# One planned order of instructions exchanged for another in a fused attention and SoLU kernel, with one GpSimd subtraction cut in two

## Chip, cores and metric

The kernel runs on one core of one Trainium2 chip. The metric is the device time of one execution in microseconds (us). Before the change it is 658.14 us, the median of 3 runs (658.04 to 658.26).

## What is computed

For 8 batches of 8 heads, 576 tokens and 64 features, causal attention with a decay that is summed along the sequence, and behind it a layer of width 1024 for each of the 4608 tokens:

```python
scores = scale * np.matmul(q, k.transpose(0, 1, 3, 2))
cum = np.cumsum(np.log(np.clip(f, 0.0001, 1.0)), axis=-1)
scores = np.where(causal, -1e9, scores + cum[:, :, :, None] - cum[:, :, None, :])
attn = softmax(scores)                      # with 1e-9 added to the sum
x = (attn @ v) as 4608 x 512                # all heads of a token side by side
h = x @ w_in                                # 512 -> 1024
solu = h * softmax(h)
ln = (solu - mean(solu)) / sqrt(var(solu) + 1e-6) * g_ln
out = ln @ w_out                            # 1024 -> 512
```

## The kernel before

**The pieces.** The 64 heads are worked on as 32 pairs (pair p is heads 2hp and 2hp+1 of batch p // 4). A pair's queries are cut into 5 tiles: 64 tokens, and four of 128. Query tile i sees the first 64 + 128 i keys, so scores are 64, 192, 320, 448 and 576 columns wide (the last in two parts of 288). Tiles 0 to 2 are "half 0" of a pair (320 tokens), tiles 3 and 4 "half 1". The layer works on 36 tiles of 128 tokens, numbered 0 to 35.

**High and low words.** Nearly every product is made from f16 words: an operand is split into a high word and the remainder, and three products (high by high, low by high, high by low) are added up. The first pairs are done in f32.

**One pair.** TensorE (PE) makes the scores in PSUM (`score_products`, L822, and L820 for the decay). VectorE (DVE) adds the mask and takes each row's maximum (L843), ScalarE (ACT) takes the exponential with its sum (L848), GpSimd (POOL) prepares the sum (L854), DVE its reciprocal (L855). ACT or POOL writes the high word of the normalized row (L504, L506), DVE the low one (L876), a transposing DMA from the SP queue turns both (L513), and PE multiplies with v (`values`, L925). ACT and DVE split that result into the two words of x (L935, L936).

**One layer tile** (`layer`). PE makes h in 8 steps of three 512-column products each (`product_in`, L956 to L958) into `hps`, two PSUM banks of which there is one copy. DVE takes the maximum (L967, L968), ACT the exponential (L970), DVE weighs it (L974); from then on `hps` is free for the next tile. POOL and ACT work out the variance (L978 to L980, L984, L988, L989), POOL normalizes (L994), ACT writes z's high word (L504), POOL subtracts to get the lower word (L998, 1024 columns in one instruction), a transposing DMA turns z, and PE makes 8 more steps of three products (`product_out`, L1026 to L1028). ACT evicts (L1058), SP stores. The names in the text: in7 is `product_in` of tile 7, out7 its `product_out`; one step of either is three products.

**What sets the order.** The Python code only records operations (`Plan.op`), each with its engine, an estimate of its duration, what it reads and writes. `Plan.schedule` then lists them: at every turn it takes, for each engine, the ready operation with the smallest rank in the table `RANK` (3576 numbers), and appends the one that can begin first. Each engine executes its part of that list in order. Where the model expects PE to stand idle and `FILLED` has a share for that time, blank products of 256 columns go into the gap (L1151); they are computed on nothing and keep PE busy. Six PSUM banks (`ps`) go round among scores, transposes, values and outputs.

```python
Z_LO = (3,) * 36                                   # 3 is POOL
op(Z_LO[n], {DVE: 1280, POOL: 2130}[Z_LO[n]], at, lambda: engine(Z_LO[n]).tensor_tensor(
    z16[:, :, 1], e2, z16[:, :, 0], ALU.subtract), [ek, zk_], [(*zk_, "l")], port=True)
FILLED = ((0.0, 300.0, 1.0), (690.0, 1000.0, 0.8)) # from, to in us of the plan, share to fill
best[e] = min((x for x in ready if x[0] <= t), key=lambda x: (x[1].due - ..., x[1].seq))
```

**The start.** The weights `w_in` come in four parts, each read as bits and split by ACT, DVE and POOL (L583, L597, L603, L619), while pairs 0 to 3 run their half 0. in0 needs half 0 of all four pairs. ACT also takes sums of squares of v (L684 on `vraw`) and of q and k (L684 on `raws`) of a batch, from which the scales of that batch's words are made; the first `raws` squared are those of batch 2.

Of the kernel before, what the change touches and what calls it, by code (L numbers as in the profile page):

```python
# [46 lines left out]
AFTER = (205.0, 135.0, 170.0, 70.0, 100.0)  # L47
# [9 lines left out]
TURN = (1100.0, 25.0, 1700.0, 6.0)  # L57
KEEP = 0.0
FILLED = ((0.0, 300.0, 1.0), (690.0, 1000.0, 0.8))
# [5 lines left out]
LANES = 8  # L65
WAIT = (0.0, 250.0, 60.0, 200.0, 0.0)

WHOLE, SCORE, TURNS, HALVES = range(4)
SWITCH = ((0.0, 120.0, 0.0, 120.0), (120.0, 0.0, 120.0, 120.0), (0.0, 120.0, 0.0, 120.0), (120.0, 120.0, 120.0, 0.0))
# [7 lines left out]
class Op:  # L77
    __slots__ = ("eng", "ns", "fn", "due", "deps", "users", "take", "keys", "left", "ready", "end", "tail", "seq", "dense", "port", "form", "layer")


class Plan:
# [10 lines left out]
    def op(self, eng, ns, due, fn, reads=(), writes=(), take=None, clear=(), tail=0.0, dense=True, port=False, form=0):  # L92
# [3 lines left out]
        o.eng, o.ns, o.fn, o.take, o.tail, o.seq, o.dense = eng, ns, fn, take, tail, len(self.ops), dense  # L96
        o.due = RANK[o.seq]
# [17 lines left out]
    def schedule(self):  # L115
        free, wire, order, gone, self.held = [0.0] * 5, 0.0, [], {}, {}
        form, port, half_clock, worked, lanes = 0, 0.0, True, 0.0, [0.0] * LANES
        todo = [[] for _ in range(5)]
        for o in self.ops:
            o.left, o.ready, o.users = len(o.deps), 0.0, []  # L120
            for d in o.deps:
                d.users.append(o)
            if not o.left:
                todo[o.eng].append(o)
        best = [None] * 5
        stale = set(range(5))
        for _ in self.ops:
            for e in stale:
                ready = []
                for o in todo[e]:  # L130
                    r = max(o.ready, free[e], port if o.port else 0.0)
                    if o.take:
                        places = self.pools[o.take[0][0]]
                        if len(places) < len(o.take):
                            continue
                        r = max(r, sorted(places)[len(o.take) - 1][0])
                    ready.append((r, o))
                best[e] = None
                if ready:
                    t = min(r for r, _ in ready) + WAIT[e]  # L140
                    best[e] = min((x for x in ready if x[0] <= t), key=lambda x: (x[1].due - (KEEP if e == PE and x[1].form == form else 0.0), x[1].seq))
            t, o = min((x for x in best if x), key=lambda x: x[0])
            stale = {PE, ACT, DVE, POOL, o.eng}
            todo[o.eng].remove(o)
            for k in o.take:
                place = min(self.pools[k[0]])
                self.pools[k[0]].remove(place)
                self.place[k] = place[1]
            self.place.update(zip(o.take, sorted(self.place[k] for k in o.take)))
            if o.eng == SP:  # L150
                t = max(t, lanes.pop(0))
                free[SP] = t + max(450.0, o.tail)
                wire = max(wire, t + 600.0) + o.ns
                o.end = max(t + 1900.0, wire + (TURN[2] if o.tail else 1300.0))
                lanes.append(o.end)
            else:
                ns = o.ns
                if o.eng == PE:
# [9 lines left out]
                free[o.eng] = t + ns  # L168
                o.end = t + ns
                if o.port:  # L170
                    port = o.end
# [1024 lines left out]
```

## Time and profile before

| | before |
|---|---|
| median of 3 runs | 658.14 us (658.04 to 658.26) |
| span of the profiled execution | 655.3 us |
| PE busy | 629.9 us (96%) |
| DVE busy | 553.4 us (84%) |
| ACT busy | 513.4 us (78%) |
| POOL busy | 400.5 us (61%) |
| DMA moved | 110.79 MB |

The span runs from the first instruction to the last of one execution that was recorded. That execution's own time is not given apart from its span; against the median of the timed runs it leaves 2.84 us that lie outside the span. A matmul's recorded end is modelled and lies about 0.16 us behind the start of the next, so a PE that is busy by the record can still hide short waits.

### The profile page before, as it was taken

How to read it: one execution, taken by the hardware profiler on the slowest of the kernel's cores; microseconds unless marked ns; L12 is line 12 of the kernel's file. 1: busy time of each engine (PE TensorE's matmuls, PEld its weight loads, DVE VectorE, ACT ScalarE, POOL GpSimd, SP SyncE). 2: the span in 40 equal slices, each digit the busy share in tenths (PEclk: the TensorE clock that was granted, in tenths of full speed). 3: DMA queues.
4: the chain of work that ended last, by engine and by line, in shares of the span. 5: the costliest groups of instructions: out<-in, count | busy, mean ns of one | idle time of the engine just before them, and what ended most of it. 6: DMA issues, size and time to landing. Idle time of an engine off the chain costs nothing. (4 is left out here: it accounts for less than half of the span.)

```text
span 655.3 us, 17355 instructions
## 1 busy us (share of the span) xinstructions
PE 629.9 (96%) x6312; PEld 343.7 (52%) x6312; DVE 553.4 (84%) x1644; ACT 513.4 (78%) x1290; POOL 400.5 (61%) x625
## 2 busy tenths in 40 slices
PE   5989999999999999999999999999999999999998
PEld 4655655555544456455455545555544554554445
DVE  6977999999999999999899888999999987874222
ACT  6998858978986987989888797888788887664433
POOL 3575762476767746876666667786677745555530
PEclk8999999999999999999999999999999999999999
DMA  8856128949897998999998989999769888686341
GB/s 338 332 176 221 55 65 207 176 76 227 185 197 150 193 230 138 206 171 214 185 214 199 187 146 210 217 181 191 148 96 167 150 155 126 138 148 129 74 97 48
DMA packets 262709, 110.79 MB, mean 169 GB/s; under 512 B 248288, under 2 KB 248736, under 8 KB 261600
## 3 DMA queue, kind: packets, MB, share of 16 engines
q1 hardware_dynamic: 262624, 109.69, 78.4%
q8 instruction: 49, 0.80, 0.5%
q14 instruction: 36, 0.29, 0.1%
HBM read 38.27 MB, written 9.66 MB: 73 GB/s over the span
## 5 line engine op out<-in xcount | busy, mean ns | idle before, releaser
L848 ACT ACTIVATE p<-p,nm 128x448 f32<-128x448 f32 (+4 forms) x208 | 132.8, 640 | 24.2 <-DVE nm L843 23.7
L956 PE MATMUL hps<-wi_h,x_h 128*128 128x512 f16 x288 | 109.8, 381 | 4.1 <-DVE e L974 3.8
L822 PE MATMUL ps<-qk 64*128 64x288 f16 (+9 forms) x1056 | 103.4, 306 | 10.4 <-DMA qk<-in_qk_dram 6.1
L957 PE MATMUL hps<-wi_l,x_h 128*128 128x512 f16 x288 | 109.3, 380 | 0.0
L958 PE MATMUL hps<-wi_h,x_l 128*128 128x512 f16 x288 | 109.3, 380 | 0.0
L1026 PE MATMUL ps<-wo_f,zz 128*128 128x512 f16 x280 | 106.7, 381 | 0.8 <-DMA zz<-z 0.8
L1027 PE MATMUL ps<-wo_f,zz 128*128 128x512 f16 x280 | 106.3, 380 | 0.0
L1028 PE MATMUL ps<-wo_f,zz 128*128 128x512 f16 x280 | 106.3, 380 | 0.0
L854 POOL TENSOR_SCALAR sm<-sm 128x2 f32<-128x2 f32 (+1 forms) x128 | 40.7, 318 | 105.7 <-ACT p L848 68.3
L843 DVE CUSTOM_DVE_ANT_0 p<-ps,mask 128x320 f32<-128x320 f32 (+4 forms) x208 | 96.7, 496 | 4.2 <-PE ps L820 2.2
L876 DVE SCALAR_TENSOR_TENSOR wo_p<-p,ri,wo_p 128x576 f16<-128x576 f32 (+1 forms) x112 | 95.3, 873 | 3.8 <-ACT wo_p L504 2.0
L998 POOL TENSOR_TENSOR z<-e,z 128x1024 f16<-128x1024 f32 x32 | 69.8, 2181 | 22.7 <-ACT z L504 22.1
L925 PEld LDWEIGHTS <-v 128*64 128x64 f16 x2520 | 70.0, 110 | 17.6 <-issue 15.9
L925 PE MATMUL ps<-t_p,v 128*64 128x128 f16 (+1 forms) x2520 | 77.0, 219 | 1.7 <-DMA t_p<-p16s 1.2
L967 DVE TENSOR_REDUCE st<-hps 128x1 f32<-128x1024 f32 x36 | 43.7, 1215 | 28.1 <-PE hps L958 28.0
L970 ACT ACTIVATE e<-hps,st,unscale 128x1024 f32<-128x1024 f32 x32 | 38.4, 1201 | 20.9 <-DVE st L968 19.1
L506 POOL TENSOR_SCALAR wo_p<-p,ri 128x576 f16<-128x576 f32 x56 | 45.2, 812 | 15.5 <-DVE ri L855 14.6
L974 DVE SCALAR_TENSOR_TENSOR e<-hps,e 128x1024 f32<-128x1024 f32 x36 | 43.7, 1214 | 11.1 <-ACT e L970 11.0
L822 PEld LDWEIGHTS <-qk 64*128 64x128 f16 x864 | 32.7, 94 | 36.1 <-issue 24.8
L820 PE MATMUL ps<-crow,pick 64*128 64x448 bf16 (+1 forms) x360 | 51.4, 276 | 0.0
L956 PEld LDWEIGHTS <-x_h 128*128 128x128 f16 x288 | 28.0, 97 | 39.9 <-issue 11.9
L984 ACT ACTIVATE junk<-e,st 128x1024 bf16<-128x1024 f32 x36 | 41.3, 1147 | 8.7 <-DVE e L974 8.5
(188 smaller groups left out, 1315.5 us busy)
## 6 DMA issues: line engine op xcount, KB each, us to landing
raws<-in_qk_dram SPq DMA_DIRECT2D x24, 576.0 KB, 4.9
vraw<-in_v_dram SPq DMA_DIRECT2D x8, 1280.0 KB, 7.2
out_dram<-y SPq DMA_DIRECT2D x35, 256.0 KB, 2.6
qk<-in_qk_dram SPq DMA_DIRECT2D x8, 576.0 KB, 8.7
wo_raw<-in_w_in_dram SPq DMA_DIRECT2D x4, 1024.0 KB, 8.1
vraw<-in_w_out_dram SPq DMA_DIRECT2D x2, 1024.0 KB, 5.0
t_raw<-in_w_out_dram SPq DMA_DIRECT2D x2, 1024.0 KB, 4.9
t_p<-p16s SPq DMA_TRANSPOSE x84, 3.5
```

The source lines that it names most:

```text
L822: nc.tensor.matmul(dst, x[row(h), 0, q0:q0 + P], y[row(h), 1, cols], start=(n == 0), stop=False)
L843: op(DVE, R_NS[i] if n == 0 else 442, at[i][h] + STEPS[0], lambda i=i, h=h, n=n, a=a, e=e, x=x, m0=m0: nc.vector.tensor_tensor_reduce(home ...
L848: op(ACT, E_NS[i] + (0 if banked(p, i) or i == 4 else 28), at[i][h] + STEPS[1], lambda i=i, h=h, x=x: nc.scalar.activation(home(i, h), hom ...
L876: op(DVE, L_NS[j], at[j][g] + STEPS[4], lambda j=j, g=g, nq=nq, h16=h16, l16=l16, r1=r1: nc.vector.scalar_tensor_tensor(l16(), home(j, g, ...
L925: nc.tensor.matmul(o[row(h), a:a + n], v16[m][:, x, 2 * j + h], t[:, y, i + j if h else i - j], start=(j == 0 and c == 0), stop=(j == i an ...
L956: nc.tensor.matmul(hps[:, sl], x_h, wi_h[:, c, sl], start=(c == 0), stop=False)
L957: nc.tensor.matmul(hps[:, sl], x_h, wi_l[:, c, sl], start=False, stop=False)
L958: nc.tensor.matmul(hps[:, sl], x_l, wi_h[:, c, sl], start=False, stop=(c == NCC - 1))
L998: op(Z_LO[n], {DVE: 1280, POOL: 2130}[Z_LO[n]], at, lambda: engine(Z_LO[n]).tensor_tensor(z16[:, :, 1], e2, z16[:, :, 0], ALU.subtract), [ ...
L1026: nc.tensor.matmul(o, zz[:, a, 0, j], wo(0, k), start=(k == 0), stop=False)
L1027: nc.tensor.matmul(o, zz[:, a, 0, j], wo(1, k), start=False, stop=False)
L1028: nc.tensor.matmul(o, zz[:, a, 1, j], wo(0, k), start=False, stop=(k == NFC - 1))
```

## The change

1. `RANK` is gone. A table `ORDER` of 3716 numbers lists all operations; `schedule` cuts it into one fixed row per engine and goes through the rows with a new model of times. The model now has a delay for every pair of engines (`LATE_BY`), durations by operation (`TRACED`), a model of the DMA ring (`RING`, `ISSUE`), and one of DVE and POOL excluding each other for operations marked `port` (`BEHIND`, `HOLD`).
2. The subtraction for z's lower word is two POOL operations of 512 columns.
3. The three small POOL operations of `sums` and the two of `deviation` are recorded one by one, so that others can stand between them. They are the same instructions.
4. `FILLED` is 0 to 13.5 us in full and 13.5 to 60 us at 0.75; blank products are 135 (before 138).

```diff
-AFTER = (205.0, 135.0, 170.0, 70.0, 100.0)
+LATE_BY = ((205.0, 205.0, 205.0, 205.0, 205.0), (165.0, 135.0, 135.0, 180.0, 135.0), ...)
-FILLED = ((0.0, 300.0, 1.0), (690.0, 1000.0, 0.8))
+FILLED = ((0.0, 13.5, 1.0), (13.5, 60.0, 0.75))
-        o.due = RANK[o.seq]
+        o.hold = HOLD[eng == POOL] if ns > 360.0 or eng == DVE else ns
+        o.ns = TRACED.get((eng, round(ns, 1)), ns)
...
-                    best[e] = min((x for x in ready if x[0] <= t), key=lambda x: (x[1].due - ..., x[1].seq))
+        for n in ORDER:
+            rows[self.ops[n].eng].append(self.ops[n])
+                o = row[0]
+                t = max([free[e], *(d.end + (SAME[e] if d.eng == e != SP else LATE_BY[d.eng][e]) for d in o.deps)])
...
-            op(Z_LO[n], {DVE: 1280, POOL: 2130}[Z_LO[n]], at, lambda: engine(Z_LO[n]).tensor_tensor(z16[:, :, 1], e2, z16[:, :, 0], ALU.subtract),
-               [ek, zk_], [(*zk_, "l")], port=True)
+            for a in range(2):
+                op(POOL, 1085, at, lambda a=a: nc.gpsimd.tensor_tensor(z16[:, a, 1], e2[:, a], z16[:, a, 0], ALU.subtract), [ek, zk_], [(*zk_, "l", a)])
```

The products and their operands, the DVE and ACT instructions and the DMAs are the same; what differs is where they stand. Three places:

**ACT, in the start**, around the squares of `raws` (L684, now L695); `p` are exponentials of pairs 1 and 2, `t` copies of transposed tiles, `x_h` high words of x. Before:

```order
L848 ACTIVATE p_64,sm_94<-p_64,nm_86 128x192
L684 ACTIVATE junk,top_113<-raws 128x1152
L935 ACTIVATE x_h<-ps_145,scale_117 128x320
L684 ACTIVATE junk,top_113<-raws 128x1152 x2
L504 ACTIVATE t_1_p<-ps_145 128x256
```

Now:

```order
L859 ACTIVATE p_64,sm_94<-p_64,nm_86 128x192 x2
L946 ACTIVATE x_h<-ps_150,scale_117 128x320
L515 ACTIVATE t_1_p<-ps_147 128x384
L515 ACTIVATE t_1_p<-ps_150 128x256
L859 ACTIVATE p_65,sm_95<-p_65,nm_87 128x320 x2
```

Three of the four squares stood here and the fourth eleven rows further on; all four now stand behind the exponential of layer tile 0.

**DVE, layer tile 14**, from the maximum (L968, now L979) to the weighing that frees `hps` (L974, now L985); `wo_p`, `p16s` are words of attention rows. Before:

```order
L968 TENSOR_SCALAR st_143<-st_143,unscale_128 128x1
L855 RECIPROCAL ri_90<-sm_94 128x2
L787 SCALAR_TENSOR_TENSOR v_3_82<-vraw_76,scale_121,v_3_82 128x640
L876 SCALAR_TENSOR_TENSOR p16s_84<-p_65,ri_90,p16s_84 128x320
L876 SCALAR_TENSOR_TENSOR wo_p_1255<-p_67,ri_89,wo_p_1255 128x576 x2
L876 SCALAR_TENSOR_TENSOR p16s_84<-p_65,ri_90,p16s_84 128x320
L936 SCALAR_TENSOR_TENSOR x_l<-ps_150,x_h 128x320
L974 SCALAR_TENSOR_TENSOR e_102,st_143<-hps,e_102 128x1024
```

Now:

```order
L979 TENSOR_SCALAR st_143<-st_143,unscale_128 128x1
L866 RECIPROCAL ri_90<-sm_94 128x4
L854 ISA p_66,nm_86<-ps_145,mask 128x448
L854 ISA nm_86 128x1
L854 ISA p_66,nm_86<-ps_147,mask 128x448
L854 ISA nm_86 128x1
L887 SCALAR_TENSOR_TENSOR wo_p_1250<-p_67,ri_89,wo_p_1250 128x576
L985 SCALAR_TENSOR_TENSOR e_102,st_143<-hps,e_102 128x1024
```

Six long instructions stood between; now there are three.

**POOL, layer tile 4**, from the normalization (L994, now L1001) on; `sm` are sums of exponentials, `v` a word of v. Before:

```order
L994 TENSOR_SCALAR e_102<-e_102,st_143 128x1024
L854 TENSOR_SCALAR sm_93<-sm_93 128x2
L998 TENSOR_TENSOR z_104<-e_102,z_104 128x2x512
L854 TENSOR_SCALAR sm_94<-sm_94 128x4
L506 TENSOR_SCALAR wo_p_1255<-p_67,ri_89 128x576
```

Now:

```order
L1001 TENSOR_SCALAR e_102<-e_102,st_143 128x1024
L1006 TENSOR_TENSOR z_104<-e_102,z_104 128x512
L865 TENSOR_SCALAR sm_93<-sm_93 128x2
L1006 TENSOR_TENSOR z_104<-e_102,z_104 128x512
L797 TENSOR_SCALAR v_3_82<-vraw_76,scale_119 128x640
```

The subtraction is in two, and the small sum of pair 4 has moved in between. In 18 of the 32 layer tiles that go this way, something stands between the halves.

## Rows read from the trace of the kernel before

**Rows 1.** The page's head: span, and each engine's busy time.

```profile
span 655.3 us, 17355 instructions
...
PE 629.9 (96%) x6312; PEld 343.7 (52%) x6312; DVE 553.4 (84%) x1644; ACT 513.4 (78%) x1290; POOL 400.5 (61%) x625
```

**Rows 2.** Busy time by stretch: length, engines, granted clock, DMA share.

```profile
core 0: us, PE busy (x) PEld busy (x) DVE busy (x) ACT busy (x) POOL busy (x), PEclk, DMA share, GB/s
13.70:18.70 5.00, 4.92 (x35) 3.30 (x36) 4.83 (x15) 4.81 (x9) 1.79 (x4) 0.50 1.01 407
...
20.00:49.40 29.40, 26.85 (x273) 18.56 (x268) 24.56 (x90) 28.59 (x84) 20.32 (x39) 1.00 0.66 235
...
60.00:100.00 40.00, 40.00 (x320) 24.33 (x317) 39.09 (x120) 29.01 (x70) 25.64 (x46) 1.00 0.27 90
60.00:500.00 440.00, 431.16 (x4513) 230.87 (x4510) 416.22 (x1265) 370.57 (x952) 291.25 (x438) 1.00 0.86 173
500.00:548.00 48.00, 45.72 (x557) 25.12 (x555) 41.16 (x134) 38.98 (x112) 29.76 (x42) 1.00 0.84 145
548.00:655.30 107.30, 104.05 (x825) 54.23 (x819) 51.67 (x115) 53.13 (x99) 46.34 (x69) 1.00 0.53 109
```

**Rows 3.** The same view for the blank products (L1151) alone: PE, PEld, clock.

```profile
0.00:13.70 13.70, 6.29 (x40) 4.72 (x40) 0.93 0.84 322
...
60.00:160.00 100.00, 4.04 (x29) 2.51 (x29) 1.00 0.60 138
```

**Rows 4.** Whom PE waited for, 60 to 548 us: total, times, longest.

```profile
PE hps L956 <- DVE e L974: 3.8, 4, 1.3
PE ps L822 <- DVE nm L843: 1.9, 4, 1.2
PE ps L822 <- ACT y L1058: 1.7, 1, 1.7
PE ps L925 <- DMA t_p<-p16s: 1.2, 2, 0.9
```

**Rows 5.** PE's timeline at five places: start, length, what, [idle before].

```profile
55.22 0.38 PE L956 MATMUL hps<-wi_h,x_h 128*128 128x512 f16 x1
...
198.59 1.12 PE L925 MATMUL ps<-t_p,v 128*64 128x64 f16 x36
199.65 0.39 PE L1026 MATMUL ps<-wo_f,zz 128*128 128x512 f16 x1
...
205.04 0.38 PE L956 MATMUL hps<-wi_h,x_h 128*128 128x512 f16 x1 [1.34 <-DVE e L974]
...
205.69 0.38 PE L956 MATMUL hps<-wi_h,x_h 128*128 128x512 f16 x1
...
309.27 0.38 PE L1028 MATMUL ps<-wo_f,zz 128*128 128x512 f16 x1
309.58 0.26 PE L822 MATMUL ps<-qk 64*128 64x64 f16 x6
...
312.73 0.72 PE L822 MATMUL ps<-qk 64*128 64x448 f16 x5 [1.66 <-ACT y L1058]
```

**Rows 6.** ACT's groups between 20 and 49.4 us: the squares of `raws`.

```profile
L684 ACT ACTIVATE junk<-raws 128x1152 bf16<-128x1152 f32 x4 | 4.6, 1158 | 0.0
```

**Rows 7.** DVE's groups by shape: busy us, mean ns of one, idle before.

```profile
L876 DVE SCALAR_TENSOR_TENSOR wo_p<-p,ri,wo_p 128x576 f16<-128x576 f32 x56 | 53.0, 968 | 1.4 <-POOL wo_p L506 1.4
...
L777 DVE SCALAR_TENSOR_TENSOR qk<-raws,scale,qk 128x576 f16<-128x576 f32 x48 | 41.3, 873 | 0.0
```

**Rows 8.** Four lines by themselves: least/median/largest ns of one.

```profile
L876 DVE SCALAR_TENSOR_TENSOR wo_p<-p,ri,wo_p x112: 655/801/2691, 103.9 to 595.5; 128x448 f16<-128x448 f32 x56, 128x576 f16<-128x576 f32 x56
...
L777 DVE SCALAR_TENSOR_TENSOR qk<-raws,scale,qk x48: 782/806/1675, 138.2 to 518.5; 128x576 f16<-128x576 f32 x48
...
L998 POOL TENSOR_TENSOR z<-e,z x32: 2122/2132/2619, 149.3 to 632.3; 128x1024 f16<-128x1024 f32 x32
...
L854 POOL TENSOR_SCALAR sm<-sm x128: 191/192/1647, 20.0 to 589.4; 128x2 f32<-128x2 f32 x96, 128x4 f32<-128x4 f32 x32
```

More of the change, by code (lines that the diff above doesn't have):

```diff
@@ L77 @@
 class Op:
-    __slots__ = ("eng", "ns", "fn", "due", "deps", "users", "take", "keys", "left", "ready", "end", "tail", "seq", "dense", "port", "form", "layer")
+    __slots__ = ("eng", "ns", "fn", "deps", "users", "take", "keys", "left", "ready", "end", "tail", "seq", "dense", "port", "form", "layer", "blocks", "hold")
 class Plan:
@@ new lines, in schedule @@
+        rows = [[] for _ in range(5)]
+        for n in ORDER:
+            rows[self.ops[n].eng].append(self.ops[n])
+        free, port, order, gone, last, self.held = [0.0] * 5, [0.0] * 5, [], {}, {}, {}
+        form, half_clock, worked, lanes, ring, drained = 0, True, 0.0, [0.0] * LANES, [], 0.0
+        for o in self.ops:
+            o.end = None
+        for _ in self.ops:
+            best = None
+            for e, row in enumerate(rows):
+                if not row or any(d.end is None for d in row[0].deps):
+                    continue
+                o = row[0]
+                t = max([free[e], *(d.end + (SAME[e] if d.eng == e != SP else LATE_BY[d.eng][e]) for d in o.deps)])
+                if o.take:
+                    places = sorted(self.pools[o.take[0][0]])
+                    if len(places) < len(o.take):
+                        continue
+                    t = max(t, places[len(o.take) - 1][0])
+                for k in o.keys:
+                    t = max([t, *(x + LATE_BY[f][e] for f, x in last.get(k, {}).items() if f != e)])
+                if o.port:
+                    t = max(t, port[POOL if e == DVE else DVE])
+                when = t + (BEHIND if o.port and e == POOL else 0.0)
+                if best is None or when < best[0]:
+                    best = when, t, o
+            _, t, o = best
+            e = o.eng
+            rows[e].pop(0)
+            for k, place in zip(o.take, sorted(n for _, n in sorted(self.pools["s"])[:len(o.take)])):
+                self.place[k] = place
+            for place in sorted(self.pools["s"])[:len(o.take)]:
+                self.pools["s"].remove(place)
+            if e == SP:
+                t = max(t, lanes.pop(0))
+                n, ns, issued = (o.blocks, o.blocks * RING[1], ISSUE[0] + ISSUE[1] * o.blocks + (ISSUE[2] if o.blocks > 128 else 0.0)) if o.tail else (max(1.0, o.ns / 120.0), o.ns * RING[2], ISSUE[3])
+                since = max(t + RING[3], drained)
+                drained = since + ns
+                ring = ring[-11:] + [(since, drained, n)]
+                free[SP], many = t + issued, 0.0
+                for a, z, n in reversed(ring):
+                    if many + n > RING[0]:
+                        free[SP] = max(free[SP], z - (RING[0] - many) / n * (z - a))
+                        break
+                    many += n
+                free[SP] += ISSUE[4]
+                o.end = drained + RING[4]
@@ L822, in products @@
                             nc.tensor.matmul(dst, x[row(h), 0, q0:q0 + P], y[row(h), 1, cols], start=(n == 0), stop=False)
[L823 removed]
+        ns = 8 + sum((16 if near else 10 if p < NAT * NPAIR else 8) * ((5.0 if p < NAT * NPAIR else 1.4) + 0.2084 * (cuts(i)[1 + (a > 0)] - a)) for i, a in pieces)
         op(PE, ns, at, products, [*((x, m, j) for x in ("qk", "qkl") for j in range(2)), *(("crow", a2, h) for h in range(2) if not near),
@@ L1138, in tile_kernel @@
     with tc.manual_schedule():
-        order, idle, busy = plan.schedule(), [], 8000.0
+        order, idle = plan.schedule(), []
+        busy = plan.writer[("const",)].end + LATE_BY[POOL][PE]
         for t, o in order:
```

113 lines of the change are left out of this document (35 added, 78 removed), and 289 rows, old and new, of tables (ORDER, RANK).

## The prediction, made before the changed kernel ran

> **What bounds the kernel.** I read the page's head first: of a span of 655.3 us PE is busy 629.9, DVE 553.4 [rows 1]. Averages over unlike stages don't say which engine to ask, so next the busy time by stretch [rows 2]. Three stages stand out. From 20 to 49.4 us ACT is busy 28.59 of 29.40 us: it sets the pace, and DVE has 4.84 us to spare there. From 60 to 500 PE is busy 431.16 of 440 and DVE 416.22: PE binds, and DVE is so close behind that PE stops wherever DVE is late. From 548 to the end PE is busy 104.05 of 107.3, and the missing 3.25 us are the last eviction and store: nothing but layer products, which an order can't shorten.
>
> So the end is PE's work plus the time in which PE does nothing useful. That time is of three kinds: the start, until in0 at 55.22 us [rows 5]; blank products, 4.04 us between 60 and 160 [rows 3]; and waits between 60 and 548, (440 - 431.16) + (48 - 45.72) = 11.1 us [rows 2], whose owners the list of waits names [rows 4].
>
> The useful work is the same after the change: row for row, every engine has as many instructions of each kind, except 3 fewer blanks and 32 more on POOL. Only idle time, blanks and the cost of switching can move, and whatever is moved changes the time about one for one. A change under 0.2% (1.3 us) I call no change, since a measurement can hardly tell it.
>
> **The start.** Four squares of `raws` leave ACT's saturated stretch: 4.6 us busy, plus four reads of the sum that mostly lie beside other work [rows 6]. Behind 60 us they cost nothing, since ACT is busy 29.01 of 40 us there [rows 2]; were that cover gone, 4.6 us. Nobody needs them early: they feed the scales of batch 2. SP loads two of the four `raws` later to match, behind the parts of w_out, past no transfer that in0 needs. What is late next is DVE: it can follow by its 4.84 idle us at most. Bounds 0 and -4.8; I take **-4.0**, near the upper end, because ACT has no idle time before the squares and DVE must do the same work to reach in0.
>
> Ahead of the first scores PE now gets 79 blanks instead of 40. Before, it stood idle after them and the granted clock from 13.70 to 18.70 was 0.50, the 1.2 GHz level, with PE busy 4.92 of 5.0 us [rows 2, 3]. If the clock stays up, up to 2.5 us of PE time fall away; but ACT (4.81 of 5.0) and DVE (4.83) are full in the same stretch and hide it: 0.
>
> **Blanks.** The other 56 stand before in0, and none behind 60 us. The 4.04 us between 60 and 160 fall away where PE would not have waited anyway. Bounds 0 and -4.0; **-2**, half, for want of a row that tells them apart.
>
> **Waits for `hps`**, 3.8 us in four places [rows 4]. in n+1 can't begin until DVE has weighed tile n. I listed what PE does between the end of in n and in n+1 at these four. One step of a layer takes 0.65 us (205.04 to 205.69), a half 0 of values 1.06 (198.59 to 199.65) [rows 5]; scores and half 1 of values I price by their columns at the same speed, as estimates.
>
> - After in6: 8 steps, tile-4 scores and a scale before; now also a half 0 of values and tile-1 scores: 7.1 to 8.7 us.
> - After in7: 8 steps and a half 0 before; now 8 steps, a half 1 and two sets of scores: 6.3 to 8.3.
> - After in14: 7.8 to 8.8.
> - After in25: 6 steps and a half 1 before, 8 steps and a half 1 now: 5.5 to 6.8.
>
> Each gains more than the mean wait of 0.95 us. After in14 DVE itself also gets to the weighing with three long instructions ahead of it instead of six. Bounds 0 and -3.8; **-3.0**.
>
> **The wait for a bank.** PE stood 1.66 us inside pair 17's 448-column scores until ACT had evicted out11's result [rows 5]. These scores now stand 8 steps of in14 and a half 1 of values later, some 6.8 us: **-1.5** (0 to -1.7).
>
> **Other waits**, 11.1 - 3.8 - 1.7 = 5.6 us. I can't follow them one by one through the new order; the bounds are -5.6 and +4. On average more PE work now stands between a half 0's last scores and its values (25.0 us against 21.4, by the same prices), but pair 30 has it cut from 16.5 to 10.3. **-1.5**.
>
> **Switching.** From a layer product to other work costs 0.31 us (309.27 to 309.58 [rows 5]) where a product otherwise takes 0.22. The order has 94 such exits to scores or values before, 77 now: 17 x 0.09 = **-1.5** (0 to -1.5).
>
> **New waits.** Handovers of `hps` become tighter after in19 (9.4 to 6.3 us), in26 (17.2 to 12.0) and in31 (5.2 to 4.7). At 0.95 us for a wait [rows 4], I take two: **+2**, with 0 and eight (+8) as bounds.
>
> **The halves.** DVE operations with two operands in SBUF are held up when POOL works: the 576-column L876 takes 968 ns on average, L777 of the same shape 873 [rows 7], while the median of the latter is 806 and single L876 reach 2691, about one L998 (2132) over its normal time [rows 8]. That is (968 - 806) x 56 + (873 - 806) x 48 = 12.3 us of DVE's time. L998 is the longest thing that POOL does, so halving it can give back 6 us at most; I expect 3. It gets no term of its own: it shortens DVE, and where that shows at the end it is in the waits above.
>
> The Trainium skill ("SBUF — State Buffer", section "SBUF: two separate sides") says why: VectorE and GpSimd share a port pair under an exclusive lock for a whole instruction, not by splitting bandwidth. The 2691 ns agree. By that rule the halves are worth their 3 us of DVE, at most 643.6 us if all of it reached the end; by shared bandwidth nothing, and the sum stays as below.
>
> For POOL the halves cost a second fixed price, of which the nearest row is the smallest sum, 0.19 us [rows 8]: 32 x 0.19 = 6.1 us of an engine that is busy 61% [rows 1]. A longer way of z to its product is hidden by the PE work between in n and out n, 18 us or more in each of the 32 tiles by the same prices.
>
> **The sum.** -4.0 - 2 - 3 - 1.5 - 1.5 - 1.5 + 2 = -11.5. That is against the profiled execution: 655.3 - 11.5 = 643.8 us of span. The median of the runs is 2.84 us above that span; I keep the difference: **646.6 us**. With all good ends it is -21.4 (636.7), with the bad ends of new and other waits and nothing gained +12.
>
> **Rivals.**
>
> 1. *The start is caught up.* DVE is busy 94.6% from 60 to 500; if it can't run 4 us further ahead, PE waits for it in small pieces later. The time is 650.6. For it speaks rows 2, against it that DVE itself idles in the start. 0.17.
> 2. *The waits move.* In-order rows make as many new waits as they remove; only start and switching stay: 655.3 - 5.5 + 2.84 = 652.6. For it: pair 30; against: at the four named places the added work exceeds the wait. 0.12.
> 3. *It doesn't do what it says.* The new model is no truer than the old, the gain in the start is given back as well: 658.1. Against it speaks that the ACT rows show a real relief. 0.08.
> 4. *Slower, by the halves.* When POOL has let go after the first half, DVE begins an operation of 0.81 us (L777's median) and the second half waits for it: 0.81 + 0.19 = 1.0 us per tile. Behind it on POOL stand the small sums on which reciprocals, words, transposes and values depend. In 18 of 32 tiles other POOL work stands between the halves as well. From 13 tiles in which PE feels the full 1.0 us, the sum of 11.5 and the bound of no change are eaten; with 18 it is 646.6 + 18 = 664.6. For it: POOL's smallest sum takes up to 1647 ns instead of 191 [rows 8]; against it: POOL has 39% idle, and the same hold-up ended later behind one long subtraction. 0.13.
>
> The lock of the skill's page cuts both ways here: by it DVE's wait is shorter and POOL's second half waits. That is what rivals 4 and the 3 us above price from rows.
>
> **Numbers.** The forecast has 0.50, by itself 641 to 652. Faster by over 0.2%: forecast and rivals 1 and 2, 0.79; same: rival 3, 0.08; slower: rival 4, 0.13. The range of 638 to 657.5 leaves out rival 4, half of rival 3 and a few in a hundred below: 0.2.
>
> **What would show it.** in0 at 51 to 52 us instead of 55.22, with ACT free of squares before it; the granted clock at its upper level from 13.7 to 18.7; waits of PE for `hps` under 1 us in sum, none over 1.5 for an evicted bank; mean L876 of 576 columns under 920 ns and none over 2000; PE idle between 55 and 550 us under 8 us. I am wrong if in0 comes earlier and the last values of the last pair don't, if the list of waits has new owners of over 5 us, or if L876 stays at 968.

## The result and the profile after

The changed kernel takes 653.2 us, the median of 20 runs (649.2 to 659.6); the kernel before, run beside it 20 times, took 658.15 (655.6 to 661.0). The ratio is 0.9915, 95% interval 0.9899 to 0.9932: 4.5 to 6.6 us faster. One of the 20 runs, the 659.6, counts as slow and is left out of the ratio; the other 19 have a median of 652.6. Forecast were 646.6 us, 11.5 less than before. The direction was right and the time lies inside the range, but less than half of the forecast gain came. The time is nearly that of rival 2 (652.6), though not by its sum: that rival kept the gain of the start, and the start gained nothing.

The profiled execution of the changed kernel spans 650.6 us. Lines stand some 11 lower than before (L822 is now L833, L876 L887, L956 L967, L998 L1006). The page's head, to be held against [rows 1]:

```profile
span 650.6 us, 17346 instructions
...
PE 624.8 (96%) x6309; PEld 345.1 (53%) x6309; DVE 543.8 (84%) x1644; ACT 512.9 (79%) x1290; POOL 400.7 (62%) x657
```

PE is busy 5.1 us less and DVE 9.6 less. The busy time by stretch, columns as in [rows 2], with three stretches added in which the clock is low or PE stands:

```profile
13.70:18.70 5.00, 3.68 (x43) 2.67 (x43) 4.47 (x17) 4.24 (x12) 2.61 (x12) 1.00 1.02 400
...
22.40:26.20 3.80, 3.80 (x32) 2.76 (x31) 1.99 (x7) 2.45 (x4) 1.07 (x2) 0.55 0.88 320
20.00:49.40 29.40, 25.54 (x252) 17.97 (x253) 23.68 (x84) 23.32 (x70) 17.37 (x33) 0.94 0.47 167
60.00:548.00 488.00, 475.08 (x5102) 258.59 (x5099) 450.94 (x1401) 415.32 (x1079) 318.95 (x502) 1.00 0.87 174
449.40:452.20 2.80, 0.72 (x5) 0.26 (x4) 1.91 (x9) 2.80 (x6) 0.19 (x1) 1.00 1.16 229
452.40:455.90 3.50, 3.50 (x10) 1.31 (x9) 3.22 (x16) 2.82 (x10) 1.34 (x3) 0.52 1.04 197
```

ACT fell from 28.59 to 23.32 us between 20 and 49.4, as the step on the squares says. The clock from 13.7 to 18.7 is at its upper level here (in a second profile of the same kernel it is 0.66). But between 60 and 548 PE stands 488 - 475.08 = 12.9 us, where it stood 11.1 before. For whom, in the list of waits (60 to 548 us, columns as in [rows 4]):

```profile
PE ps L653 <- DVE top L648: 3.5, 3, 2.1
PE ps L936 <- DMA t_p<-wo_p: 1.9, 2, 1.1
PE ps L678 <- DVE scale L676: 1.3, 2, 0.8
PE ps L833 <- ACT y L1065: 1.3, 2, 1.1
PE ps L936 <- DVE qk L788: 1.3, 1, 1.3
...
PE hps L967 <- DVE e L985: 0.4, 1, 0.4
```

The owner of [rows 4], `hps`, is down from 3.8 to 0.4, and most of what stands above it is new. Three places of PE's timeline (columns as in [rows 5]): the first scores of pair 1, in0, and the longest wait.

```profile
22.21 0.52 PE L833 MATMUL ps<-qk 64*128 64x64 f32 x4 [1.20 <-DMA qk<-in_qk_dram]
...
56.14 0.38 PE L967 MATMUL hps<-wi_h,x_h 128*128 128x512 f16 x1
...
451.88 0.49 PE L653 MATMUL ps<-ident,top 128*1 128x128 f32 x3 [2.08 <-DVE top L648]
```

in0 comes at 56.14, not at 51 to 52, and in this profile later than before (55.22 [rows 5]). The blank products, PE's part of the view of [rows 3], first before and then after, by sums:

```profile
sum 655.30, PE 20.93 PEld 13.71; mean PE 6.98 PEld 4.57
```

```profile
sum 650.60, PE 19.17 PEld 13.63; mean PE 6.39 PEld 4.54
```

Now the 4.7 us of span can be laid out without remainder. PE's own products: 629.9 - 20.93 = 608.97 before, 624.8 - 19.17 = 605.63 after, so -3.3. Blanks: -1.8 (none are left behind 60 us). PE standing still: 655.3 - 629.9 = 25.4 before, 650.6 - 624.8 = 25.8 after, so +0.4. What the order was to save in waits is not there; the time for the products themselves got shorter.

DVE's two groups and four single lines that answer to [rows 7] and [rows 8]:

```profile
L887 DVE SCALAR_TENSOR_TENSOR wo_p<-p,ri,wo_p 128x576 f16<-128x576 f32 x56 | 47.3, 855 | 2.4 <-POOL wo_p L517 2.3
...
L788 DVE SCALAR_TENSOR_TENSOR qk<-raws,scale,qk 128x576 f16<-128x576 f32 x48 | 40.6, 850 | 0.0
```

```profile
L887 DVE SCALAR_TENSOR_TENSOR wo_p<-p,ri,wo_p x112: 650/800/1572, 103.4 to 596.6; 128x448 f16<-128x448 f32 x56, 128x576 f16<-128x576 f32 x56
...
L1006 POOL TENSOR_TENSOR z<-e,z x64: 1152/1158/1784, 147.8 to 626.1; 128x512 f16<-128x512 f32 x64
...
L865 POOL TENSOR_SCALAR sm<-sm x128: 192/193/854, 18.4 to 590.9; 128x2 f32<-128x2 f32 x96, 128x4 f32<-128x4 f32 x32
```

968 ns became 855, the longest L876 of 2691 ns became 1572, and a POOL sum takes at most 854 ns where it took up to 1647.

### The profile page after: what moved, and what is told of

Read it like the earlier page. It is cut to its first block, busy times and chain, and to the rows that moved or that the text cites. A ratio compares the mean times of both kernels' runs of the same rounds, so it can differ in the third digit from the quotient of the medians.

```text
span 650.6 us, 17346 instructions
## 1 busy us (share of the span) xinstructions
PE 624.8 (96%) x6309; PEld 345.1 (53%) x6309; DVE 543.8 (84%) x1644; ACT 512.9 (79%) x1290; POOL 400.7 (62%) x657
## 4 chain that ended last, share of the span: by engine, by line
PE 57%; DVE 14%; DMA 10%; ACT 6%; POOL 6%; issue 4%; SPq 1%; ACTq 0%; DVEq 0%; POOLq 0%
PE ps L833 8%; PE hps L967 7%; PE hps L969 6%; PE hps L968 6%; PE ps L1033 6%; PE ps L936 6%; PE ps L1035 6%; PE ps L1034 6%; DVE p L854 4%; DMA raws<-in_qk_dram 3%; DMA qk<-in_qk_dram 2%; DMA t_p<-wo_p 2%; PE ps L831 2%; DVE p16s L887 2%; DVE wo_p L887 2%
## 5 line engine op out<-in xcount | busy, mean ns | idle before, releaser
L854 DVE CUSTOM_DVE_ANT_0 p<-ps,mask 128x448 f32<-128x448 f32 (+4 forms) x208 | 99.6, 496 | 12.9 <-PE ps L831 7.7
L967 PE MATMUL hps<-wi_h,x_h 128*128 128x512 f16 x288 | 109.6, 380 | 0.4 <-DVE e L985 0.4
L968 PE MATMUL hps<-wi_l,x_h 128*128 128x512 f16 x288 | 109.3, 380 | 0.0
L833 PE MATMUL ps<-qk 64*128 64x288 f16 (+9 forms) x1056 | 101.5, 305 | 5.2 <-DMA qk<-in_qk_dram 2.8
L865 POOL TENSOR_SCALAR sm<-sm 128x2 f32<-128x2 f32 (+1 forms) x128 | 35.9, 280 | 112.2 <-ACT p L859 79.4
L1006 POOL TENSOR_TENSOR z<-e,z 128x512 f16<-128x512 f32 x64 | 78.0, 1228 | 23.0 <-ACT z L515 20.7
L887 DVE SCALAR_TENSOR_TENSOR wo_p<-p,ri,wo_p 128x448 f16<-128x448 f32 (+1 forms) x112 | 88.2, 801 | 3.9 <-POOL wo_p L517 2.3
L517 POOL TENSOR_SCALAR wo_p<-p,ri 128x576 f16<-128x576 f32 x56 | 44.6, 801 | 9.1 <-DVE ri L866 7.4
L985 DVE SCALAR_TENSOR_TENSOR e<-hps,e 128x1024 f32<-128x1024 f32 x36 | 43.7, 1214 | 7.0 <-ACT e L981 6.9
L833 PEld LDWEIGHTS <-qk 64*128 64x128 f16 x864 | 32.6, 94 | 31.2 <-issue 20.9
L967 PEld LDWEIGHTS <-x_h 128*128 128x128 f16 x288 | 28.1, 97 | 39.2 <-issue 10.1
L1033 PEld LDWEIGHTS <-zz 128*128 128x128 f16 x280 | 27.5, 98 | 36.9 <-issue 7.3
```

What stands on the lines that cost most here:

```text
L833: nc.tensor.matmul(dst, x[row(h), 0, q0:q0 + P], y[row(h), 1, cols], start=(n == 0), stop=False)
L854: op(DVE, R_NS[i] if n == 0 else 442, at[i][h] + STEPS[0], lambda i=i, h=h, n=n, a=a, e=e, x=x, m0=m0: nc.vector.tensor_tensor_reduce(home ...
L887: op(DVE, L_NS[j], at[j][g] + STEPS[4], lambda j=j, g=g, nq=nq, h16=h16, l16=l16, r1=r1: nc.vector.scalar_tensor_tensor(l16(), home(j, g, ...
L967: nc.tensor.matmul(hps[:, sl], x_h, wi_h[:, c, sl], start=(c == 0), stop=False)
L968: nc.tensor.matmul(hps[:, sl], x_h, wi_l[:, c, sl], start=False, stop=False)
L1006: op(POOL, 1085, at, lambda a=a: nc.gpsimd.tensor_tensor(z16[:, a, 1], e2[:, a], z16[:, a, 0], ALU.subtract), [ek, zk_], [(*zk_, "l", a)])
```

## Experiments

In most runs a few operations were moved and nothing else. A pair (n, m) takes operation n out of the recorded order and puts it directly behind operation m; numbers are those of the recording, and the words beside each diff name them. All times are medians of 6 to 12 executions, all ratios are to the kernel before on the same chip. The place of in0 is that of one execution, the profiled one.

**The changed kernel once more.**

> The changed kernel once more, unedited, as the neighbour of the three edits run beside it on the same chip. Every theory expects it within 0.3% of 653.2 us, with in0 again at about 56 us and pair 1's first scores at about 22 us. Should in0 come at 51 to 52 us here, the first profile was an exception and the failed start would be no fact.

653.4 us, ratio 0.9928 (0.9903 to 0.9954), in0 at 56.30. In a third profile of it (below) in0 came at 54.89. Over all seven profiles of kernels with the changed start (this one and edits that act later) in0 lies at 54.9 to 56.9 us, over five with the old start at 55.0 to 55.8. So the start gained nothing, as a fact; that it lost 0.9 us is one pair of profiles.

### The start

**Were the squares the start's bound?** The kernel before with the four squares of `raws` moved on ACT:

```diff
+MOVED = ((972, 428), (971, 462), (974, 583), (975, 582))
```

> The kernel before with nothing but the four squares of raws moved out of the start on ACT, to four places behind the exponential of layer tile 0. The prediction's step: ACT sets the pace of the start, so in0 comes at 51 to 52 us instead of 55.2 and the time falls by 2.5 to 4 us. Rival H, the start hangs on a chain that goes round ACT, VectorE, GpSimd and PE, and an engine that is full on that chain is not yet its bound: in0 at 54 to 55.5 us, the time within 1 us of before.

657.2 us, ratio 0.9999 (0.9983 to 1.0014). The stretch from 20 to 49.4 us and in0:

```profile
20.00:49.40 29.40, 26.96 (x268) 18.43 (x266) 24.43 (x91) 24.35 (x77) 20.66 (x40) 1.00 0.67 238
```

```profile
55.07 0.38 PE L956 MATMUL hps<-wi_h,x_h 128*128 128x512 f16 x1
```

ACT has 4.24 us less to do, and in0 moves by 0.15. This is the prediction's largest single term, tried alone, and it is worth nothing. DVE stays at 24.43 of 29.4 us: it did not follow. An engine that is 97% busy was not what the start waited for.

**What holds the start of the changed kernel?** In SP's row the load of pair 1's qk stands behind v and g_ln (issued at 5.92 us, before at 4.76), and pair 2's behind the store of the running sums, for which SP waits until 16.5 (issued at 17.67, before at 9.84). Three rows of SP's timeline, after:

```profile
5.92 1.79 SPq L521 DMA_DIRECT2D qk<-in_qk_dram  x1
...
16.52 0.47 SPq L521 DMA_DIRECT2D c_scratch<-t_cc  x1
...
17.67 1.04 SPq L521 DMA_DIRECT2D qk<-in_qk_dram  x1
```

First only pair 1's load (operation 35) went back behind the last part of w_in (44):

```diff
+MOVED = ((35, 44),)
```

> The changed kernel with one load moved on SP: qk of pair 1 directly behind the last part of w_in, as it stood before the change, ahead of v and g_ln. Theory A, the start failed because of this late load: pair 1's first scores come at 19.5 to 20.5 us instead of 22.2, in0 at 53 to 54 us instead of 56.1, and the time falls by 2 to 3.5 us against the unedited changed kernel. Rival B, the start is held later on by GpSimd's row (the bits of w_out ahead of pair 3's exponentials at 42.5 to 45.8 us) and by the return trips between the engines: the first scores come early, in0 stays at 55.3 us or later, the time moves by less than 1 us.

652.7 us, ratio 0.9910 (0.9886 to 0.9934); pair 1's scores at 21.25 us and in0 at 57.30. Theory A in this form fell: the scores came a microsecond earlier and in0 didn't. The chain of waits went over POOL instead, where the preparation of g_ln waited for the small load that was now one place later, with pair 0's exponentials behind it:

```profile
22.74 0.20 POOL L576 TENSOR_SCALAR gs<-g_sb 128x8 f32<-128x8 f32 x1 [2.74 <-DMA g_sb<-in_g_ln_dram]
```

So L576 (33) was put behind the sums of pair 2 (175) as well:

```diff
+MOVED = ((35, 44), (33, 175))
```

> The changed kernel with the qk load of pair 1 early again, and GpSimd's preparation of g_ln (L576) behind the sums of pair 2 instead of ahead of pair 0's exponentials, where GpSimd stood until 22.7 us for that small load in the run with the early load alone. Theory B, the start is a chain of rows in order, and this was its next link: pair 0's exponentials are scaled from 20 us on, in0 at 53 to 55 us, 1 to 2.5 us less than the unedited changed kernel. Rival H, there is a third and a fourth link behind it (bits of w_out, squares of w_out): in0 at 55.5 us or later and no change over 1 us.

652.2 us, ratio 0.9915 (0.9883 to 0.9947), in0 at 56.18: rival H. The chain now went over pair 2's load, the one behind the store:

```profile
26.75 0.44 PE L833 MATMUL ps<-qk 64*128 64x64 f32 x4 [1.07 <-DMA qk<-in_qk_dram]
```

With the loads of pairs 2 and 3 (36, 37) ahead of that store too:

```diff
+MOVED = ((35, 44), (36, 32), (37, 36), (33, 175))
```

> The run with the early load and the late g_ln, and also the qk loads of pairs 2 and 3 ahead of the store of the running sums on SP, for which SP stood until 16.5 us with pair 2's load behind it. Theory B, the loads in SP's row were the links of the start's chain: pair 2's scores by 24.5 us instead of 26.7, in0 at 52.5 to 54.5 us, 1 to 3 us less than the changed kernel (0.9895 to 0.9910 of before). Rival H: another link takes over, in0 at 55.5 us or later, 0.991 to 0.993 of before.

648.9 us, ratio 0.9883 (0.9848 to 0.9918): the fastest of all the kernels here. in0 comes at

```profile
53.78 0.38 PE L967 MATMUL hps<-wi_h,x_h 128*128 128x512 f16 x1
```

Beside the unedited changed kernel on one chip:

> The changed kernel, unedited, on the same chip as the next run, as its neighbour: 0.990 to 0.994 of before.

> The run with the qk loads of pairs 1 to 3 early and g_ln late once more, beside the unedited changed kernel on one chip, since their intervals against before touched. If the loads are what the start lost, its median lies 2 to 5 us below the neighbour's and in0 at 53.5 to 54.5 us again; if the first result was a chip or a lucky granted clock, within 1 us of the neighbour.

651.5 us without the edit (ratio 0.9921, 0.9896 to 0.9945) and 650.3 with it (0.9894, 0.9870 to 0.9918); in0 at 54.89 and 53.77. The place of in0 came back to a hundredth, 1.1 us ahead of the earliest of the seven profiles without the edit. The gain of time is 1.1 us between these medians, 1.8 between these ratios and 3.0 between those of the first run with these loads early and of the changed kernel once more, so for the most part less than the 2 to 5 expected here. The intervals overlap: 1 to 3 us is my estimate, and that the time fell is likely but not shown. Nor is shown what holds in0 at 53.8 instead of 51 to 52; the last longer wait of PE before it is for GpSimd's scaled exponentials (L517), 1.03 us up to 50.73. The preparation of g_ln moved along in both runs and was not tried apart from the loads.

The same three loads moved back in the kernel before, with its squares where they were:

```diff
+MOVED = ((35, 32), (36, 26), (37, 36))
```

> The kernel before with the qk loads of pairs 1 to 3 as late on SP as the change has them: pair 1 behind v and g_ln, pairs 2 and 3 behind the store of the running sums. Theory B: pair 1's scores at 21 to 22.5 us instead of 19.6, in0 at 57 to 59 us and 1.5 to 3.5 us more than before, which is what the change lost there while ACT was relieved. Rival: the old order has room for it, in0 within 1 us of 55.2 and the time within 0.7 us.

662.5 us, ratio 1.0084 (1.0050 to 1.0118), 5.5 us slower. Pair 1's scores and in0:

```profile
22.69 0.44 PE L822 MATMUL ps<-qk 64*128 64x64 f32 x4 [2.25 <-DMA qk<-in_qk_dram]
```

```profile
60.27 0.38 PE L956 MATMUL hps<-wi_h,x_h 128*128 128x512 f16 x1
```

Theory B held, and with more than it asked: three loads a few places later in one queue cost 5.05 us of in0. It is no copy of the changed kernel's rows: pair 1's load was issued at 7.92 us (5.92 there) and pair 2's at 19.63 (17.67 there), since loads of `raws` stand ahead, and behind the wait the granted clock was 0.50 from 24 to 30 us, which is part of the 5 us. So the size does not carry over, the direction does. Relief of ACT that alone is worth nothing, and loads that came later, are why the start did not gain.

One link more was tried: the second early bits of w_out on POOL (238) behind pair 3's first scaled exponentials, with its followers:

```diff
+MOVED = ((35, 44), (36, 32), (37, 36), (33, 175), (238, 222), (239, 147), (241, 239), (240, 241), (248, 239))
```

> The run before with the second of the early bits of w_out (2.06 us on GpSimd) behind pair 3's sums and first scaled exponentials, and its followers on VectorE, ACT and SP moved behind it. Theory B: pair 3's exponentials are scaled 1 to 2 us earlier, in0 1 to 2 us earlier than in the run with the loads alone, and the time as much less. Rival: the words of w_out come as much later and PE waits for them behind in0: same time within 0.7 us.

654.9 us, ratio 0.9966 (0.9944 to 0.9988): 5.5 us worse by the ratios than the same without it, with in0 at 59.06. ACT's square of w_out (L743) now waited 1.82 us for words that came later, with an exponential of pair 0 behind it and POOL's sums behind that, and PE stood longer at the same place, with a low clock after it:

```profile
53.79 0.36 PE L906 MATMUL ps<-ident,p 64*128 64x64 f32 x1 [2.36 <-POOL p L517]
```

```profile
52.00:58.00 6.00, 4.21 (x31) 3.36 (x32) 1.46 (x3) 3.00 (x8) 4.14 (x5) 0.50 0.81 298
```

**Do the more numerous blanks ahead matter?** Only 40 ahead of the first scores:

```diff
+if t < 13500.0:
+    ahead.append(many)
+    many = max(0, min(many, 40 - sum(ahead[:-1])))
```

> The changed kernel with only 40 blank products ahead of the first scores; of the 92 that its plan lays before 13.5 us the rest is left out. Theory A expects the granted clock from 13.7 to 18.7 us back at or near 0.5, its first scores up to 2 us slower, and no change of the time over 1 us, since the start waits for a load until 22 us anyway. The rival, that the blanks are what keeps the start from being still later: in0 at 57 to 59 us and 1 to 3 us more.

653.0 us, ratio 0.9924 (0.9897 to 0.9951), the same as with all. The granted clock from 13.7 to 18.7 was 0.50 again and in0 came at 57.93, but the end did not move: the zero that the prediction put down for the clock there holds. It also shows that a later in0 is not handed on to the end one for one, as the prediction had it for whatever is moved: in0 1.6 us later cost nothing here, and 1.0 later with pair 1's load alone cost nothing either.

### Waits and blanks

**The term for `hps` alone.** In the kernel before, PE work was put ahead of the next tile where PE had waited for `hps`. A first form had one place more, where pair 18's first scores went into a bank that other work still used, so that it computes something else, and it brought 25 more blanks:

> The kernel before with PE work put between two layer tiles at the four places where PE waited for hps: two score tiles ahead of in7, the large score tile and three steps apart ahead of in8, one score tile ahead of in15, two steps of out23 ahead of in26. The prediction's term: the waits for hps fall from 3.8 to under 1 us and the time by 2.5 to 3.5 us. Rival F, the time goes to other waits: under 1 us less, with waits of other owners that grow.

659.1 us, ratio 1.0025 (1.0007 to 1.0042): it can't tell, for the blanks. Without that place, and with blanks as before:

```diff
+MOVED = ((910, 1133), (938, 1169), (939, 938), (940, 939), (941, 940), (2658, 2598), (2599, 2598))
```

> The kernel before with PE work put ahead of the next layer tile at three of the four places where PE waited for hps (two score tiles ahead of in7, the large score tile ahead of in8, two steps of out23 ahead of in26); blank products stay as many as before. The prediction's term: the waits for hps fall by 2.5 to 3.3 us and the time by 2 to 3.3 us. Rival F, waits change their owner: the waits for hps fall, the time by less than 1 us.

658.3 us, ratio 1.0015 (0.9993 to 1.0037). Its list of waits:

```profile
PE ps L822 <- DVE nm L843: 2.8, 5, 1.3
PE ps L925 <- DMA t_p<-p16s: 1.6, 1, 1.6
PE ps L822 <- ACT y L1058: 1.5, 1, 1.5
PE ps L822 <- DVE p16s L876: 1.3, 1, 1.3
PE hps L956 <- DVE e L974: 0.5, 1, 0.5
```

The waits for `hps` fell by 3.3 us and the time by nothing: rival F, in part. Other waits grew by some 2 us (PE stands 488 - 478.05 = 9.95 us from 60 to 548, 11.1 before), and from 180 to 200 us the granted clock was 0.91 in this profile, by that share 1.8 us. That DVE, busy 457.4 of 488 us there before and 456.5 now, is behind the waits that grew is argued, not shown.

**Blanks alone.** The kernel before without its 31 blanks behind 60 us:

```diff
-for _ in range(many):
+for _ in range(many if t < 60000.0 else 0):
```

> The kernel before without its 31 blank products behind 60 us. The prediction's term: 2 us less (0 to 4). Rival: the blanks stood only where PE would have waited anyway, and the time stays within 1 us; or the granted clock falls below 1.00 in a stretch between 60 and 200 us, where it was 1.00, and the time rises by 1 to 2 us.

658.1 us, ratio 1.0011 (0.9997 to 1.0024), against -2 in the prediction. Where blanks were, PE now waits 1.7 us for the scales, and the clock fell once, by its share 1.8 us; together nearly the 4.04 us that the blanks took:

```profile
PE ps L667 <- DVE scale L665: 1.1, 1, 1.1
PE ps L642 <- DVE top L637: 0.6, 1, 0.6
```

```profile
120.00:140.00 20.00, 17.15 (x178) 9.79 (x178) 17.25 (x63) 16.12 (x51) 9.55 (x20) 0.91 0.61 118
```

**The changed kernel's longest waits.** The transposes of squared sums, two and four steps later at 179 and 452 us, by drawing those steps ahead:

```diff
+MOVED = ((2638, 2637), (2315, 2638), (2316, 2315), (2317, 2316), (2318, 3233), (2319, 2318), (2320, 2319), (861, 910), (862, 861))
```

> The changed kernel with the transposes of squared sums (L653) two and four steps of a layer later on PE at two places (179 and 452 us), where PE waited 1.2 and 2.1 us for them; nothing else is moved. Theory E, a wait of the new order is lost time one for one, and behind the longer one the granted clock falls as well (0.91 from 440 to 460 us): 2.5 to 5 us less than the unedited changed kernel, clock 1.00 from 440 to 460 us, no wait at L653 over 0.5 us. Rival F, waits only change their owner: less than 1 us less, with other waits that grow by 2 us or more.

653.4 us, ratio 0.9931 (0.9907 to 0.9956): no gain. The wait at L653 fell from 3.5 to 0.2, and the clock was 1.00 from 440 to 460 as theory E says, but:

```profile
PE ps L833 <- ACT y L1065: 3.0, 2, 2.7
PE ps L678 <- DVE scale L676: 2.5, 4, 0.9
PE ps L936 <- DVE scale L684: 1.7, 1, 1.7
```

Rival F once more: PE stands 14.4 us from 60 to 548, against 12.9. The squares themselves are late at 452 us in the changed kernel (ACT waited 2.4 us for a load of `raws` that landed at 448.0), and moving who waits for them doesn't make them earlier.

### The halves and the switches

**One subtraction instead of two**, in the changed kernel, at the first half's place:

```diff
-nc.gpsimd.tensor_tensor(z16[:, a, 1], e2[:, a], z16[:, a, 0], ALU.subtract)
+a or nc.gpsimd.tensor_tensor(z16[:, :, 1], e2, z16[:, :, 0], ALU.subtract)
```

> The changed kernel with z's lower word as one GpSimd subtraction again, at the place of its first half. Theory C, the halves shorten VectorE's hold-ups: the mean of the 576-column products of L887 goes from about 900 ns to 940 to 970, single ones over 2000 ns come back, VectorE is 4 to 8 us busier, and 1 to 3 us of that reach the end. Rival D, the halves cost GpSimd more than they give (0.19 us a tile, 6 us): the time falls by up to 2 us. If what the order saves is all that counts, the time stays within 0.7 us.

655.5 us, ratio 0.9965 (0.9942 to 0.9989), against 653.4 of the changed kernel on the same chip: the halves are worth 2.0 us there, theory C. The two intervals overlap by 0.0012, so the size is loose; DVE's own time, below, is not. Between 60 and 548 us:

```profile
60.00:548.00 488.00, 472.87 (x5096) 257.82 (x5093) 456.66 (x1400) 414.16 (x1077) 312.94 (x476) 1.00 0.86 174
```

PE stands 15.1 us against 12.9 with the halves, DVE is busy 456.66 against 450.94. Single products of over 2000 ns are back (least, median and largest as in [rows 8]):

```profile
L887 DVE SCALAR_TENSOR_TENSOR wo_p<-p,ri,wo_p x112: 649/798/2546, 103.3 to 598.7; 128x448 f16<-128x448 f32 x56, 128x576 f16<-128x576 f32 x56
```

```profile
L788 DVE SCALAR_TENSOR_TENSOR qk<-raws,scale,qk x48: 784/808/2268, 125.1 to 532.8; 128x576 f16<-128x576 f32 x48
```

The means rose less than expected: L887 of 576 columns from 860 (the changed kernel on this chip) to 869 ns, L788 from 854 to 904.

**The halves in the kernel before:**

```diff
-engine(Z_LO[n]).tensor_tensor(z16[:, :, 1], e2, z16[:, :, 0], ALU.subtract)
+[engine(Z_LO[n]).tensor_tensor(z16[:, a, 1], e2[:, a], z16[:, a, 0], ALU.subtract) for a in range(2)]
```

> The kernel before with nothing but the two halves, the second directly behind the first. Theory C, the halves free VectorE whatever the order is: VectorE 4 to 8 us less busy, L876 of 576 columns at 850 to 910 ns instead of 968, the time 1.5 to 3 us less. Rival G, the gain of the halves needs the new order, since PE in the old one waits elsewhere: within 1 us of before. Rival D, the second fixed price on GpSimd decides: 1 to 5 us more.

656.8 us, ratio 0.9986 (0.9973 to 0.9999): 0.9 us, at the edge of what can be told. DVE is 1.9 us less busy, L876 of 576 columns at 961 ns on average. The longest single one fell here too:

```profile
L876 DVE SCALAR_TENSOR_TENSOR wo_p<-p,ri,wo_p x112: 658/799/1712, 103.6 to 594.9; 128x448 f16<-128x448 f32 x56, 128x576 f16<-128x576 f32 x56
```

That is nearest to rival G; the second half stands directly behind the first here, while in the change other POOL work stands between them in 18 tiles, which may be the difference. It was not tried apart.

**Four quarters** in the changed kernel:

```diff
+[nc.gpsimd.tensor_tensor(z16[:, a, 1, c:c + 256], e2[:, a, c:c + 256], z16[:, a, 0, c:c + 256], ALU.subtract) for c in (0, 256)]
```

> The changed kernel with z's lower word in four GpSimd instructions of 256 columns in place of two of 512. Theory C, VectorE is held up by one instruction at a time: what is left of its hold-ups behind z falls, VectorE 1 to 3 us less busy, time 0 to 1.5 us less. Rival D, the fixed price on GpSimd (two more of 0.19 us a tile, 12 us in all) shows: GpSimd some 12 us busier and 1 to 3 us more time.

655.0 us, ratio 0.9975 (0.9954 to 0.9997): rival D. Its interval lies above that of the changed kernel in the result, by some 4 us between the ratios; the chips differ.

```profile
PE 626.6 (96%) x6309; PEld 346.5 (53%) x6309; DVE 544.4 (83%) x1644; ACT 512.8 (78%) x1290; POOL 413.4 (63%) x721
```

POOL is 12.7 us busier, about what 64 fixed prices of 0.19 us foretell (12.2), and DVE is no less busy. The longest L887 is still 1347 ns, and it lies beside another instruction of POOL, one that nobody cut:

```profile
L887 DVE SCALAR_TENSOR_TENSOR wo_p<-p,ri,wo_p x112: 654/801/1347, 104.2 to 599.7; 128x448 f16<-128x448 f32 x56, 128x576 f16<-128x576 f32 x56
...
460.25 1.29 POOL L797 TENSOR_SCALAR v<-vraw,scale 128x640 f16<-128x640 f32 x1
```

**The price of an exit.** 21 layer steps in the middle of their tiles one place later, behind the scores or values that followed them; the exits from layer products to any other work grow from 97 (77 of them to scores or values) to 118. The first four of the 21 pairs:

```diff
+MOVED = ((309, 454), (526, 770), (513, 698), (517, 736), ...)
```

> The changed kernel with 21 layer steps put one place later on PE, behind the scores or values that followed them, so that PE goes 21 times more from a layer product to other work; the steps are inside their tiles, so nobody waits for them alone. Theory S, each exit costs 0.09 us as the prediction has it: 1.9 us more than the unedited changed kernel; if entering the layer again costs as much, up to 3.8 us. Rival: an exit costs nothing that the end sees, within 0.7 us.

654.3 us, ratio 0.9952 (0.9933 to 0.9972), 1.6 us more than the changed kernel's 0.9928 on another chip. That agrees with 0.09 us an exit (1.9 us), but the two intervals overlap, so it isn't shown.

## Why the prediction was wrong, step by step

- **The start, -4.0: the step that failed.** It said that ACT sets the pace because it is full and nothing idles ahead of the squares. ACT became free as foretold, and in0 came no earlier (56.14 against 55.22). The squares alone are worth 0.15 us of in0 (shown in the kernel before): ACT was full, but it was not what in0 waited for. The sentence "past no transfer that in0 needs" looked at the loads of `raws` alone; on SP the qk loads of pairs 1 to 3 had moved behind others, and those are transfers that in0 needs. Late loads cost up to 5.05 us of in0 in the old order and, with the preparation of g_ln, 1.1 to 2.5 against two of the profiles in the new one; with them early in0 was at 53.8, so even then 2.6 of the 4.0 us are missing. The prediction had counted what moved on ACT, and not on SP.
- **Clock from 13.7 to 18.7, 0: right.** It rose in the first and third profile (0.66 in the second) and was worth nothing (the run with 40 blanks).
- **Blanks, -2: wrong, 0.** Without them PE waited 1.7 us more and the clock fell. By that profile they stood for the most part where PE would have waited, or kept the clock up.
- **Waits, -4.0 in sum (`hps` -3, bank -1.5, others -1.5, new +2): wrong, +1.8.** Every named wait went: `hps` 3.8 to 0.4, the 1.66 us for pair 17's bank is gone from the list. The working of each place was right and the sum was not: a wait that goes is time only if no other comes in its place. Four new owners at the head of the list come to 8.0 us (3.5 + 1.9 + 1.3 + 1.3); the prediction called itself wrong from 5 on. Others and new waits together were put at +0.5 (-1.5 and +2) and came to 12.9 - 0.4 - 5.6 = +6.9; the bounds (+4 and +8) were wide enough, the middle not.
- **Switching, -1.5: too small, or not the only cause.** PE's products took 3.3 us less, with nearly as much slow clock in both: 4.92 x 0.5 = 2.5 us in [rows 2], 3.80 x 0.45 + 3.50 x 0.48 = 3.4 after. The exits are the only cause I know; the run with 21 more is of the right size and not sharp enough. The term counted exits to scores or values alone; with those to transposes and scales PE's order has 110 before and 97 after, so 13 x 0.09 = 1.2 us. What makes up the rest of the 3.3 us stays open.
- **The halves, 3 us of DVE and no term: right on DVE, and a term was missing.** DVE gained some 5 us by them in the new order (456.66 against 450.94 and, in the second profile, 451.98 us between 60 and 548), and some 2 us reached the end. Rival 4 did not come: POOL's small sums take less than before, not more. 2 x 1158 - 2132 is 0.18 us, the fixed price as forecast.

So the order alone gives 0.9965, some 2.3 us, and the halves about 2 of the rest. That the time fell into the range all the same is partly luck: start, blanks and waits missed, and what came was from shorter products, for which the sum had -1.5, and from the halves, for which it had no term. The Trainium skill ("SBUF — State Buffer", section "SBUF: two separate sides") states that VectorE and GpSimd lock their shared port pair for a whole instruction. The halves agree: the longest excess of L876 over its median was 2691 - 801 = 1.89 us, close under one whole L998 (2132), and is now 1572 - 800 = 0.77, under one half (1158); with the whole subtraction put back it is 2546 - 798 = 1.75. In the kernel before, with halves, it is 1712 - 799 = 0.91. The quarters put a limit to it: DVE was no less busy, and its longest product then stood beside L797 (1.29 us), not beside the subtraction. What is left of the hold-ups belongs at least in part to other instructions of POOL.

## What to carry to other kernels

When rows are rewritten, list for every queue what moved past what, the loads first: a load three places later in a queue that waits for a store cost more than the fullest engine's relief gave back. A busy share of 97% shows that an engine is full, not that the end waits for it; move the work away in the old kernel and see. And price the waits beside a nearly full engine in sum, not one by one: taken away singly, in three of three runs, they gave no time; other waits or a lower clock stood in their place.

## What was not expected of the hardware

The granted clock fell in the middle of a busy kernel, with no wait of PE longer than 2.1 us. In the changed kernel PE waited 1.20 us up to 22.21 and 2.08 us up to 451.88; from 22.4 to 26.2 the clock was then 0.55, from 452.4 to 455.9 it was 0.52, that is mostly at 1.2 GHz. By these shares each fall took 1.7 us of PE's time on top of the wait (3.80 x 0.45 and 3.50 x 0.48), an estimate.

The length of the wait does not tell it. In the same profile PE waited 1.21 us up to 35.32 and 1.26 us up to 147.31, and in the kernel before 1.66 us up to 312.73 [rows 5], and behind each the clock stayed at 1.00. What differs in the rows is what PE did before: it was busy 0.63 of the 2.2 us up to 22.2 and 0.72 of 2.80 us up to 452.2. But in the second profile, with 0.79 of the same 2.2 us, the clock did not fall. After, 20 to 22.2 and behind 35.32; before, behind 312.73; and the second profile from 22.4 to 26.2:

```profile
20.00:22.20 2.20, 0.63 (x4) 0.45 (x4) 2.17 (x8) 2.20 (x7) 1.12 (x4) 1.00 1.03 415
...
35.40:38.80 3.40, 3.40 (x40) 2.28 (x40) 2.87 (x11) 2.25 (x10) 2.18 (x6) 1.00 0.00 0
```

```profile
312.80:316.50 3.70, 3.70 (x21) 1.62 (x21) 2.79 (x11) 3.63 (x13) 1.55 (x5) 1.00 1.02 187
```

```profile
22.40:26.20 3.80, 3.32 (x42) 2.49 (x40) 2.82 (x12) 3.41 (x7) 1.02 (x2) 1.00 0.89 324
```

The spread between executions of one program may be partly this; it is not shown. Over 19 runs of the changed kernel the mean granted clock lay between 0.989 and 0.997, and the time fell by 5.5 us for each 0.01 of it (a straight line through them). That is no price of the clock as such: with 40 blanks ahead all six runs had 0.982 to 0.986, and the time was 653.0 us all the same; in its profile most of the low clock lay ahead of in0 (0.50 from 13.7 to 20 us). In the fastest kernel's profile it was 1.00 from the first scores to 500 us.
